# Attention and feed-forward in one kernel: one pool of four single PSUM banks, a half tile more in seven products, and a new order of all engines

## The chip, the cores and the metric

The kernel runs on one core of a Trainium2 chip. The metric is the device time of one execution in microseconds (us), the median of the runs shown; lower is better. A profile is one execution recorded instruction by instruction; its span runs from the program's first instruction to its last.

## The reference

```python
def _attn_ref(q, k, v, bias_table):            # q, k, v: (8, 8, 576, 64); bias_table: (32, 8)
    scores = scale * np.matmul(q, k.transpose(0, 1, 3, 2))
    ...
    bucket = np.where(is_small, n, large) + np.where(rel < 0, 0, 0)   # n = |i - j|
    scores = scores + bias_table[bucket].transpose(2, 0, 1)[None, :, :, :]
    scores = scores - np.max(scores, axis=-1, keepdims=True)
    attn = np.exp(scores)
    attn = attn / (np.sum(attn, axis=-1, keepdims=True) + 1e-09)
    return np.matmul(attn, v)

def _moe_ref(x, w_in, w_out):                  # x: (4608, 512); w_in: (512, 2048); w_out: (2048, 512)
    h = x @ w_in
    g = np.maximum(0.01 * h, h)
    return g @ w_out

x = attn_out.transpose(0, 2, 1, 3).reshape(B * S, H * D)
return _moe_ref(x=x, **moe_kwargs)
```

Eight batches of eight heads go through attention with a bias that depends on |i - j| alone; its output, 4608 tokens of 512 values, goes through two matrix products with a leaky ReLU between them.

## The kernel before

**Attention.** Work goes by pairs of heads: pair n is heads 2p and 2p+1 of batch b, with n = 4b + p, 32 pairs in all. For a pair, q and k are brought to d-by-token layout, either by TensorE transposes (`turn_by_pe`, L414 and L419) or by one DMA transpose on the SP queue (`turn_by_dma`, L405, chosen by `by_dma`), and copied to `qt` and `kt` (`take_turned`, L431, on ACT or DVE). `score` makes six products u = 0 to 5 in tiles of two PSUM banks (`ps_s`); `expo` (L470 to L477) takes the exponential on ACT into `at`, `extra` or `at4`; `band` (L490) multiplies the part near the diagonal by the exponential of the bias, on DVE. `av` (L525, L528) multiplies by v with a column of ones, one head (e = 0 or 1) to a bank (`ps_o`, `ps_om`); `norm` (L537, L538) divides on DVE into `opair`. The result is turned to `xT`, by TensorE and a copy (`x_pe`, `x_copy`) or by a DMA transpose on SP (`x_dma`, L544). For pairs 4 to 30 the last 64 keys go first (`av_tail`), beside the next pair's score tiles 2 and 3.

**Feed-forward.** The 4608 tokens make nine tiles T of 512, and tile T needs all four pairs of every batch that it touches: tile 2 needs pairs 8 to 11. `ffn_in` (L576) makes one of 16 blocks f of 128 hidden values in two halves of two matmuls of 512 columns; `ffn_act` (L652) is the leaky ReLU on ACT. The second product goes by seven products of half-size blocks instead of eight, with sums formed on DVE (`mix_g`, `mix_weights`; `product`, L706; `combine`, L722 and L714). For the tiles in `SPLIT` the first product goes by seven products too, in two units u of eight blocks f each (`in_product`, L633), at the price of copies on ACT (`in_keep`, L637), additions on DVE (`in_add`, L643) and ReLUs from SBUF (`in_act`, L649).

**PSUM.** Eight banks: two score tiles of two banks ("S"), one bank for AV ("O") and three for everything else ("M").

**Order.** Every engine runs an order written at build time. `Plan` takes tasks with an engine, a cost, what they come after and which PSUM slots they take and give. It places them one by one by the earliest start and a rank, with three tables by task number: `SHIFT` changes ranks, `HOLD` delays, `SWAP` moves a copy between ACT and DVE. All engines, SP and POOL too, then run in that order, and wait for each other by semaphores. Where the plan sees TensorE idle in the first 26 us of its own reckoning, `spin` puts matmuls on a tile of zeros (`junk`). The plan reckons 6 us for an `x_dma`, and a rule of its own for `turn_by_dma`:

```python
if "turns" in t:
    t["end"] = max(r + 4.5, min(ring + 2.0, r + 11.0))
if "moves" in t:
    t["end"] = ring = max(ring, r + t["cost"] + 1.0) + t["moves"]
```

Of the kernel before, what the change touches and what calls it, by code (L numbers as in the profile page):

```python
# [10 lines left out]
FP32 = mybir.dt.float32  # L11
# [24 lines left out]

class Plan:


    LAG, COLD, WARM, EARLY, PATIENCE = 0.25, 4.9, 26.0, 34.0, 0.3  # L40

    SHIFT = {
# [26 lines left out]
    }  # L69

    SWAP = (20, 62, 88, 91, 92, 180, 185, 209, 214, 265, 273, 274, 996, 1089, 1368, 1757,)

    def __init__(self, slots):
        self.tasks = []
# [93 lines left out]
    def run(self, fill):  # L168

        for t in self.order():  # L170
            if t["engine"] == "PE" and 3.9 < t["start"] < self.WARM:
                k = round(t["idle"] / 0.22) if t["start"] < 8.5 else int((t["idle"] - 0.1) / 0.11)
                if k > 0:
                    fill(k)
# [924 lines left out]
```

## Time and profile before

| what | value |
|---|---|
| median of 3 runs | 360.63 us (360.44 to 366.01) |
| profiled execution, its own time | 360.76 us |
| its span | 359.0 us |
| mean granted TensorE clock | 0.999 |
| DVE busy, share of the span | 83% |
| ACT busy, share of the span | 73% |
| matmuls on zeros (`junk`) | 44 |
| DMA traffic | 39.58 MB |

The profiled execution takes 1.76 us more than its span, which lies around the first and the last instruction. TensorE's busy time counts a matmul from its start to the end of its drain, so that neighbours overlap; what one costs in a row of its like is the distance from start to start. In the profile's rows PE is TensorE's matmuls, DVE VectorE, ACT ScalarE, POOL GpSimd (which issues most loads) and SP the queue of DMA transposes and stores; the number in brackets at a row's end is how long the engine had been idle, and for whom it waited.

### The profile page before, as it was taken

To read this page: it belongs to the slowest core of one execution; us is meant where nothing else is said; L and a number is where in the kernel's file an instruction comes from. 1 tells how busy PE (TensorE), PEld (TensorE's weight loads), DVE (VectorE), ACT (ScalarE), POOL (GpSimd) and SP (SyncE) were. 2 spreads that over 40 slices of the span, in tenths; PEclk is the share of its full clock that TensorE was granted. 3 is DMA by queue.
4 is the path that set the end of the run, shared out by engine and by line. 5 is a ranking of instruction groups with operands and counts; after the bars stand their busy time and mean duration, and the time that the engine had idled before them with its cause. 6 is when DMAs were issued, how large, how long until landed. Compare 5 with 4: busy or idle time off the path is not lost.

```text
span 359.0 us, 9973 instructions
## 1 busy us (share of the span) xinstructions
PE 350.7 (98%) x4147; PEld 254.1 (71%) x4172; DVE 297.6 (83%) x705; ACT 262.2 (73%) x352; POOL 70.3 (20%) x107
## 2 busy tenths in 40 slices
PE   8998999999999999999999999999999999999996
PEld 5665456774677655656767777667678888888885
DVE  6897979999799968986899879999559489497593
ACT  4988999678986899797988887887933574656530
POOL 8956123080008004300700310000000000000000
PEclk9999999999999999999999999999999999999999
DMA  8999999999949987991999296411123011030033
GB/s 126 148 178 193 203 179 144 142 147 208 133 113 125 136 153 89 193 182 20 133 158 222 42 141 89 135 21 21 20 20 119 2 63 57 2 117 2 0 119 117
DMA packets 103724, 39.58 MB, mean 110 GB/s; under 512 B 83200, under 2 KB 98560, under 8 KB 103680
## 3 DMA queue, kind: packets, MB, share of 16 engines
q0 software_dynamic: 53424, 18.21, 52.8%
q1 hardware_dynamic: 49904, 20.32, 31.8%
q8 instruction: 32, 0.52, 0.6%
q10 hardware_dynamic: 352, 0.43, 0.4%
q14 instruction: 12, 0.10, 0.1%
HBM read 36.70 MB, written 9.44 MB: 129 GB/s over the span
## 4 chain that ended last, share of the span: by engine, by line
PE 90%; DVE 5%; ACT 3%; issue 1%; DVEq 0%; ACTq 0%
PE pm L706 31%; PE pm L576 21%; PE pm L633 10%; PE ps_s L456 9%; PE ps_om L525 5%; PE ps_o L525 5%; PE ps_s L460 2%; PE ps_s L463 2%; PE ps_w L1064 1%; ACT at L470 1%; DVE at L490 1%; PE ps_o L510 1%; DVE opair L538 1%; PE ps_t L414 1%; ACT gt L652 1%
## 5 line engine op out<-in xcount | busy, mean ns | idle before, releaser
L470 ACT ACTIVATE at<-ps_s 128x1024 bf16<-128x1024 f32 x124 | 121.2, 1031 | 25.4 <-PE ps_s L456 22.3
L576 PE MATMUL pm<-xT,w_in_sb 128*128 128x512 bf16 (+1 forms) x423 | 91.2, 347 | 1.5 <-DVE xT L557 0.5
L490 DVE TENSOR_TENSOR at<-at,hk 128x768 bf16<-128x768 bf16 (+4 forms) x156 | 66.6, 450 | 14.1 <-ACT at L470 11.0
L652 ACT ACTIVATE gt<-pm 128x512 bf16<-128x512 f32 x96 | 57.3, 620 | 17.0 <-PE pm L576 16.5
L576 PEld LDWEIGHTS <-w_in_sb 128*128 128x128 bf16 x448 | 40.1, 98 | 32.4 <-issue 5.5
L706 PEld LDWEIGHTS <-gt 128*128 128x128 bf16 x576 | 54.7, 98 | 11.7 <-issue 3.0
L722 DVE TENSOR_TENSOR y<-pm,y 128x512 f32<-128x512 f32 (+1 forms) x53 | 41.1, 778 | 18.1 <-PE pm L706 17.1
L268 POOL DMA_DIRECT2D vn<-in_v_dram x32 | 28.8, 912 | 126.1 <-PE ps_o L525 110.9
L706 PEld LDWEIGHTS <-sum 128*128 128x128 bf16 x432 | 41.2, 98 | 9.0 <-issue 2.5
L525 PEld LDWEIGHTS <-at 128*128 128x128 bf16 x1240 | 41.4, 98 | 3.0 <-issue 0.7
L456 PE MATMUL ps_s<-qt,kt 64*128 64x512 bf16 x256 | 40.5, 387 | 0.6 <-ACT qt L431 0.4
L706 PE MATMUL pm<-w_out_sb,gt 128*128 128x256 bf16 x288 | 36.9, 273 | 0.0
L706 PE MATMUL pm<-mix,gt 128*128 128x256 bf16 x288 | 36.2, 273 | 0.0
L706 PE MATMUL pm<-w_out_sb,sum 128*128 128x256 bf16 x288 | 36.0, 273 | 0.0
L525 PE MATMUL ps_o<-vn,at 128*128 128x65 bf16 x640 | 25.4, 193 | 0.3 <-DVE opair L538 0.2
L525 PE MATMUL ps_om<-vn,at 128*128 128x65 bf16 x600 | 24.0, 194 | 0.0
L477 ACT ACTIVATE at<-ps_s 128x576 bf16<-128x576 f32 x31 | 20.9, 673 | 0.5 <-PE ps_s L464 0.4
L643 DVE TENSOR_TENSOR at<-pm,at 128x512 f32<-128x512 f32 (+1 forms) x18 | 15.3, 864 | 6.7 <-ACT at L637 3.6
L637 ACT COPY at<-pm 128x1024 f32<-128x1024 f32 x12 | 12.1, 1012 | 12.0 <-PE pm L633 11.9
L472 ACT ACTIVATE at<-ps_s 128x512 bf16<-128x512 f32 x31 | 19.0, 613 | 2.4 <-PE ps_s L460 1.7
L456 PEld LDWEIGHTS <-kt 64*128 64x128 bf16 x256 | 8.0, 94 | 17.3 <-issue 15.8
L706 PE MATMUL pm<-mix,sum 128*128 128x256 bf16 x144 | 19.0, 273 | 0.0
(119 smaller groups left out, 505.1 us busy)
## 6 DMA issues: line engine op xcount, KB each, us to landing
out_dram<-y SPq DMA_DIRECT2D x16, 512.0 KB, 3.4
vn<-in_v_dram POOLq DMA_DIRECT2D x32, 128.0 KB, 6.4
qn<-in_q_dram POOLq DMA_DIRECT2D x14, 288.0 KB, 10.9
kn<-in_k_dram POOLq DMA_DIRECT2D x14, 288.0 KB, 11.3
w_in_sb<-in_moe_w_in_dram POOLq DMA_DIRECT2D x2, 1024.0 KB, 11.2
w_out_sb<-in_moe_w_out_dram POOLq DMA_DIRECT2D x2, 1024.0 KB, 18.9
out_dram<-y SPq DMA_DIRECT2D x3, 256.0 KB, 2.2
qn<-in_q_dram POOLq DMA_DIRECT2D x4, 144.0 KB, 4.0
```

What stands on the lines that cost most here:

```text
L268: nc.gpsimd.dma_start(out=vn[i][:, c, :, 0:D], in_=v[b, :, c * P : (c + 1) * P, :].rearrange("h s d -> s h d"),)
L456: nc.tensor.matmul(ps[:, e, :], lhsT=kt[r, u * P : (u + 1) * P], rhs=qt[r, 0:512], start=True, stop=True)
L470: nc.scalar.activation(at[:, :, u, 0:512], ps, AF.Exp, scale=scale)
L472: nc.scalar.activation(at[:, :, :, 512:S].rearrange("p e c i -> p c e i"), ps[:, 0, :].rearrange("p (c e i) -> p c e i", e=2, i=SL), AF.Ex ...
L477: nc.scalar.activation(at4[:, 0:S], ps.rearrange("p e i -> p (e i)")[:, 0:S], AF.Exp, scale=scale)
L490: nc.vector.tensor_tensor(out=o, in0=o, in1=m, op=ALU.mult)
L525: nc.tensor.matmul(ps[:, ic, :], lhsT=at[:, o : o + P], rhs=vn[i][:, c, 2 * p + e, :], start=whole and c == 0, stop=not whole and ic == NJ ...
L576: nc.tensor.matmul(pms[T, f][:, o : o + n], lhsT=w_in_sb[:, c, f * P : (f + 1) * P], rhs=xT[c][:, x : x + n], start=(c == 0 and i == 0), s ...
L633: nc.tensor.matmul(ps[:, i, :], lhsT=w, rhs=x, start=fresh and i % 2 == 0 and c == 0, stop=i % 2 == 1 and c == 1, skip_group_check=not fresh)
L652: nc.scalar.activation(gts[T][:, f, :], pms.pop((T, f)), AF.Prelu, bias=0.0, scale=1.0, alpha=0.01)
L706: nc.tensor.matmul(ps[:, ts, :], lhsT=l[:, ts * P : (ts + 1) * P], rhs=r, start=(ts == 0 or apart) and j == 0, stop=(ts == 1 or apart) and ...
L722: nc.vector.tensor_tensor(out=out_, in0=ps, in1=x, op=ALU.add)
```

## The change

- **PSUM:** the AV bank joins the others: four single banks "M" for AV, feed-forward, transposes and the rest. The two score tiles stay.
- **Seven products for half a tile more:** `SPLIT` becomes a list of units, and holds the second unit of tile 5 beside both units of tiles 6, 7 and 8.
- **Pair 7's q and k** are turned by TensorE, as those of pairs 5, 6 and 8 are, and no longer by DMA.
- **Bias table:** its last row is loaded beside the table by a second small DMA and subtracted on DVE, where a TensorE matmul into a bank (`ps_d`) did that.
- **Stores:** each tile's four blocks of 256 rows by 256 columns are stored one by one, when each is done (`block_store`); before, two stores of 256 rows by 512 columns. The first product's copy goes to block c21 instead of c22.
- **Fixed tiles:** `qt`, `pr` and `tu` become fixed buffers used in turn.
- **Zeros:** 19 spins at the start instead of 10; `heat` may put further ones into the bank that the next matmul will write. The program holds 44 of them, as before; 5 stand in an AV bank.
- **Planner:** DMA landings are reckoned with two lanes that share the engines (`Lanes`), in-products of tiles 2 and later are ordered as if their inputs landed 1.5 us later (`spare`), and the three tables are new, so that the order changes on all engines.

```diff
+class Lanes:
...
+    def push(self, t, r):
+        self.now = self.flow(self.now, max(r, self.now), self.queue, self.coming, lambda t, at: None)
+        self.coming.append((r + t["lead"], t["n"], t["lane"], t, t["moves"]))
...
-    LAG, COLD, WARM, EARLY, PATIENCE = 0.25, 4.9, 26.0, 34.0, 0.3
+    LAG, COLD, WARM, EARLY, PATIENCE, FILL = 0.25, 6.3, 26.0, 34.0, 0.3, 95.0
     SHIFT = {
-        31: 1843, 37: 293, 52: 34.5, 154: -274.5, 157: -208.5, 175: 318.5, 205: -304, 207: -210.5, 208: 10248.5,
...
+        30: 208, 53: -955, 94: 68, 147: 50, 152: 38.5, 162: 53.5, 189: 309, 209: -183, 227: 31.5, 228: 125.5,
...
-        if "turns" in t:
-            t["end"] = max(r + 4.5, min(ring + 2.0, r + 11.0))
         if "moves" in t:
-            t["end"] = ring = max(ring, r + t["cost"] + 1.0) + t["moves"]
+            ring.push(t, r)
...
+            if t["engine"] == "PE" and 6.0 < t["start"]:
+                if t["start"] < self.WARM:
+                    fill(round(t["idle"] / 0.22) if t["start"] < 9.0 else int((t["idle"] - 0.1) / 0.11))
+                elif t["start"] < self.FILL:
+                    self.pre = max(0, int((t["room"] - 0.2) / 0.11))
...
-    ps_o_pool = ctx.enter_context(tc.tile_pool(name="ps_o", bufs=1, space=bass.MemoryType.PSUM))
-    ps_m_pool = ctx.enter_context(tc.tile_pool(name="ps_m", bufs=3, space=bass.MemoryType.PSUM))
+    ps_m_pool = ctx.enter_context(tc.tile_pool(name="ps_m", bufs=4, space=bass.MemoryType.PSUM))
...
+    nc.vector.tensor_tensor(out=tab[:, 0, :], in0=tab[:, 0, :], in1=tab[:, 1, :], op=ALU.subtract)
...
-            nc.scalar.activation(diag[r, g, :], ps[r, 0:H], AF.Exp)
+            nc.scalar.activation(diag[r, g, :], tab[:, 0, :], AF.Exp)
+    def heat(ps):
+        for _ in range(plan.pre):
+            nc.tensor.matmul(ps[:, 0:256], lhsT=junk[:, 0:P], rhs=junk[:, 0:256], start=True, stop=True)
+        plan.pre = 0
...
     def by_dma(n):
-        return n > 2 * n_pairs or n == 2 * n_pairs - 1
+        return n > 2 * n_pairs
...
-            outs[n, e] = ps_o_pool.tile([P, NJ + 1, D + 1], FP32, name="ps_o", tag="ps_o")
+            outs[n, e] = ps_m_pool.tile([P, NJ + 1, D + 1], FP32, name="ps_o", tag="m")
+        heat(outs[n, e].rearrange("p i d -> p (i d)"))
...
-    def block_store(T, r, g, ss, queue):
+    def block_store(T, r, g, ss=(0, 1), queue=nc.sync):
...
-    plan = Plan({"S": 2, "O": 1, "M": 3})
+    plan = Plan({"S": 2, "M": 4})
...
-            d = add("SP", 0.1, [r0, r1] + cut.get(n - NTU, [])[:2], lambda: turn_by_dma(n), rank, tail=6.0)
+            d = moves(add("SP", 1.3, [r0, r1] + tu_use.get(n - NTU, []), lambda: turn_by_dma(n), rank), 2.2, 1, 2.0, 2.6)
...
-            xt[n] = [add("SP", 0.1, nms + free_x, lambda: x_dma(n), soon + 4, tail=6.0)]
+            xt[n] = [moves(add("SP", 1.2, nms + free_x, lambda: x_dma(n), soon + 4), 1.2, 1, 2.0, 2.6)]
...
+            if T > 1:
+                for t in early + [i]:
+                    t["spare"] = 1.5
...
-                stored[T] = [add("SP", 0.1, [cb[5], cb[4]], lambda: ffn_store(T, 1), 10000, tail=2.5)]
+                stored[T, r, g] = [moves(add("SP", 0.45, [cb[k]], lambda r=r, g=g: block_store(T, r, g), 10000), 0.75, 1, 2.0, 2.3)]
...
-    SPLIT = (6, 7, 8)
+    SPLIT = [(5, 1)] + [(T, u) for T in (6, 7, 8) for u in range(2)]
...
-    spin(10)
+    spin(19)
```

How the order moves is seen at three places. The first is VectorE's queue while the first pairs of heads are worked: `at_115` (before) and `at_112` (after) belong to pair 0, `at_116` and `at_113` to pair 1, `extra` to pair 2; a product of one of these with `hk` is a `band`, and RECIPROCAL is the start of a `norm`. Before:

```order
L490 TENSOR_TENSOR at_116<-at_116,hk 128x2x256
L490 TENSOR_TENSOR at_116<-at_116,hk 128x2x384 x2
L490 TENSOR_TENSOR at_116<-at_116,hk 128x2x320
L490 TENSOR_TENSOR at_1_118<-at_1_118,hk_102 128x192
L490 TENSOR_TENSOR at_115<-at_115,hk 128x2x320
L431 COPY qt<-ps_t 128x576
L435 TENSOR_TENSOR qt<-qt,own 128x128
L490 TENSOR_TENSOR extra<-extra,hk 128x2x256
L490 TENSOR_TENSOR extra<-extra,hk 128x2x384
L537 RECIPROCAL rcp<-ps_o 128x5
```

And the same place now:

```order
L531 TENSOR_TENSOR at_112<-at_112,hk 128x2x256
L531 TENSOR_TENSOR at_112<-at_112,hk 128x2x384 x2
L531 TENSOR_TENSOR at_112<-at_112,hk 128x2x320
L531 TENSOR_TENSOR at_0_114<-at_0_114,hk_90 128x192
L531 TENSOR_TENSOR at_113<-at_113,hk 128x2x256
L471 COPY kt_99<-ps_t 128x576
L475 TENSOR_TENSOR kt_101<-kt_101,own 128x128
L475 TENSOR_TENSOR kt_99<-kt_99,own 128x128
L531 TENSOR_TENSOR at_113<-at_113,hk 128x2x384 x2
L531 TENSOR_TENSOR at_113<-at_113,hk 128x2x320
L475 TENSOR_TENSOR qt_102<-qt_102,own 128x128
L579 RECIPROCAL rcp<-ps_o 128x5
```

Pair 0's band of 320 columns, without which its AV cannot start, stood behind all of pair 1's; now it stands ahead of pair 1's first, and pair 0's division comes ahead of pair 2's bands. On TensorE, pair 0's AV goes from behind pair 2's third score tile to behind pair 1's fifth.

The second is the SP queue around the output transposes of pairs 8 to 11 (`xT_90` to `xT_93` before, `xT_78` to `xT_81` now), on which tile 2 waits. Before:

```order
L544 DMA_TRANSPOSE xT_90<-opair 128x5x128
L405 DMA_TRANSPOSE tu<-pr 128x12x96 x2
L544 DMA_TRANSPOSE xT_91<-opair 128x5x128
L726 DMA out_dram<-y 128x2x512
L405 DMA_TRANSPOSE tu<-pr 128x12x96
L544 DMA_TRANSPOSE xT_92<-opair 128x5x128
L544 DMA_TRANSPOSE xT_93<-opair 128x5x128
```

And now:

```order
L586 DMA_TRANSPOSE xT_78<-opair 128x5x128
L445 DMA_TRANSPOSE tu_108<-pr_105 128x12x96
L769 DMA out_dram<-y 128x2x256
L586 DMA_TRANSPOSE xT_79<-opair 128x5x128
L445 DMA_TRANSPOSE tu_109<-pr_106 128x12x96
L769 DMA out_dram<-y 128x2x256
L586 DMA_TRANSPOSE xT_80<-opair 128x5x128
L445 DMA_TRANSPOSE tu_110<-pr_107 128x12x96
L586 DMA_TRANSPOSE xT_81<-opair 128x5x128
```

Pair 11's transpose now stands behind one of q and k that followed it, and narrower stores stand between.

The third is TensorE at the first in-product of tile 2. Before, it follows a product of tile 1:

```order
L706 LDWEIGHTS sum_98
L706 MATMUL pm_2414<-w_out_sb,sum_98 128x256
L576 LDWEIGHTS w_in_sb
L576 MATMUL pm_2436<-xT_90,w_in_sb 128x512
L576 LDWEIGHTS w_in_sb
L576 MATMUL pm_2436<-xT_91,w_in_sb 128x512
```

And now it follows a score tile of pair 13:

```order
L501 LDWEIGHTS kt_100
L501 MATMUL ps_s<-qt_103,kt_100 128x128
L619 LDWEIGHTS w_in_sb
L619 MATMUL pm_2384<-xT_78,w_in_sb 128x512
L619 LDWEIGHTS w_in_sb
L619 MATMUL pm_2384<-xT_79,w_in_sb 128x512
```

Between the end of pair 11's AV and this matmul TensorE's queue held pairs 12's and 13's AV before, and holds pair 12's alone now: seven half products of `product` (four matmuls each), pair 13's six score products with pair 12's tail, and pair 12's two AV heads.

More of the change, by code (lines that the diff above doesn't have):

```diff
@@ L145, in order @@
             r = max([r] + [s[t["take"].count(k) - 1] for k, s in held.items()])
-            ring = self.place(t, r, free, slots, ring)
+            t["room"] = r - max([free.get(e, 0.0)] + [s[t["take"].count(k) - 1] for k, s in held.items()])
+            self.place(t, r, free, slots, ring)
         return done
@@ L165, in place @@
             slots[k].append(t["end"] + self.LAG)
-        return ring
     def run(self, fill):
         for t in self.order():
[L171 to L174, printed above, removed]
+            if t["engine"] == "PE" and 6.0 < t["start"]:
[3 more added lines that the diff above has]
+                    self.pre = max(0, int((t["room"] - 0.2) / 0.11))
             t["go"]()
+            self.pre = 0
 @with_exitstack
@@ L248 @@
     kts_ = [per.tile([P, S + P], BF16, name=f"kt{i}") for i in range(3)]
+    qt_ = [per.tile([P, S + P], BF16, name=f"qt{i}") for i in range(3)]
+    pr_ = [per.tile([P, 2, NC, 2 * D], BF16, name=f"pr{i}") for i in range(NPR)]
+    tu_ = [per.tile([P, 2 * NC, RQ], BF16, name=f"tu{i}") for i in range(NTU)]
     own = per.tile([P, 2, SL], BF16, name="own")
@@ L427, in take_turned @@
         if j == 0:
[L428 removed]
+            t = qts[n] = qt_[n % NQT]
         else:
@@ L756, with moves, pool_load @@
     prev = []
-    def pool_load(key, cost, go, moves, after=(), rank=1):
+    def moves(t, work, lane, lead, least, yields=0.39):
+        t["moves"], t["lane"], t["lead"], t["least"], t["yields"] = work, lane, lead, least, yields
+        return t
+    def pool_load(key, cost, go, work, after=(), rank=1):
         t = add("POOL", cost, prev + list(after), go, rank)
-        t["moves"] = moves
+        moves(t, work, 0, min(cost + 1.0, 3.2), cost + 2.2, 0.39 if key[0] in ("qk", "v") else 0.2)
         prev[:] = [t]
@@ new lines, in plan_split, with pe @@
+        rank = [10000 + T * 64 + (u * 7 + i) * 64 / 14 for i in range(7)]
+        g = SPLIT.index((T, u))
+        prior = held_use[g - 2] if g >= 2 else [t for m in range(N - 2, N) for t in avt[m]]
+        def pe(k, after, r, take=(), q=None):
+            for hf in (None,) if k == 2 else (0, 1):
+                t = add("PE", 0.439, base + after, lambda hf=hf: in_product(T, u, k, q, hf), rank[r], take=list(take))
+                xm_use.setdefault(T, []).append(t)
+                after, take = after + [t], ()
+            return t
@@ new lines, in plan_split @@
+        sums = lambda k: [wm[k, c] for c in range(2)]
+        a1 = pe(1, prior + opened[-1:], 0, ["S"])
+        k1 = add("ACT", 0.91, [a1] + prior, lambda: in_keep(T, u, 0), 0)
+        bs = [pe(2, [a1], 1, ["M"], q) for q in range(2)]
+        h11 = [add("DVE", 0.605, [bs[q], k1], lambda q=q: in_add(T, u, 0, ("b", q), q), 0, give=["M"]) for q in range(2)]
+        a6 = pe(6, [k1, xm] + sums(1), 2)
+        k6 = add("ACT", 0.91, [a6] + prior, lambda: in_keep(T, u, 1), 0)
+        c5 = pe(5, [xm, a1] + sums(0), 3, ["S"])
@@ L978, in plan_ffn @@
+        held_use.append(p)
+        return {2 * j + h: ((p[0], p[3]), (p[1], p[2]))[h] for j in range(4 * u, 4 * u + 4) for h in range(2)}
     def plan_ffn(T):
```

214 lines of the change are left out of this document (104 added, 110 removed), and 40 rows, old and new, of tables (HOLD, SHIFT).

## The prediction

> **What bounds the kernel now.** I read the page's busy shares and the chain of waits first.
>
> ```profile
> span 359.0 us, 9973 instructions
> PE 350.7 (98%) x4147; PEld 254.1 (71%) x4172; DVE 297.6 (83%) x705; ACT 262.2 (73%) x352; POOL 70.3 (20%) x107
> PE 90%; DVE 5%; ACT 3%; issue 1%; DVEq 0%; ACTq 0%
> ```
>
> TensorE carries 90% of the chain, but a mean says nothing of where another engine decides. So next I read the busy times by stages (columns: stretch, its length, busy time and instructions of PE, PEld, DVE, ACT, POOL, then clock, DMA share, GB/s).
>
> ```profile
> 34.00:60.00 26.00, 24.72 (x247) 13.24 (x251) 23.35 (x62) 25.28 (x38) 7.72 (x11) 1.00 1.55 184
> 60.00:260.00 200.00, 198.85 (x2481) 135.54 (x2499) 175.79 (x444) 164.77 (x231) 36.79 (x47) 1.00 1.02 119
> 260.00:353.00 93.00, 92.95 (x872) 81.72 (x873) 68.43 (x108) 46.40 (x49) 0.00 (x0) 1.00 0.15 51
> ```
>
> From 60 to 353 us TensorE rests for 1.15 + 0.05 = 1.2 us in all. There a change pays only by taking work from TensorE, and costs only by making it wait. From 34 to 60 it rests for 26.00 - 24.72 = 1.28 us, and ACT is the fuller engine (25.28). Before 34 us TensorE's busy time says little, since matmuls on zeros fill its gaps. So there I read ACT's timeline, from the first exponential to the first of pair 4 (start, duration, line, operation, then the idle time before it and its releaser).
>
> ```profile
> 8.40 1.94 ACT L470 ACTIVATE at<-ps_s 128x1024 bf16<-128x1024 f32 x2 [1.77 <-PE ps_s L456]
> 10.54 1.94 ACT L470 ACTIVATE at<-ps_s 128x1024 bf16<-128x1024 f32 x2 [0.21 <-PE ps_s L456]
> 12.96 0.60 ACT L472 ACTIVATE at<-ps_s 128x512 bf16<-128x512 f32 x1 [0.48 <-PE ps_s L460]
> ...
> 24.58 0.65 ACT L477 ACTIVATE extra<-ps_s 128x576 bf16<-128x576 f32 x1 [0.69 <-PE ps_s L464]
> ...
> 26.30 1.94 ACT L470 ACTIVATE at<-ps_s 128x1024 bf16<-128x1024 f32 x2 [0.39 <-PE ps_s L456]
> 28.45 2.11 ACT L470 ACTIVATE at<-ps_s 128x1024 bf16<-128x1024 f32 x2 [0.22 <-PE ps_s L456]
> 30.46 0.63 ACT L431 COPY kt<-ps_t 128x576 bf16<-128x576 bf16 x1
> ...
> 33.89 1.94 ACT L470 ACTIVATE at<-ps_s 128x1024 bf16<-128x1024 f32 x2 [1.22 <-PE ps_s L456]
> ```
>
> Between 8.40 and 33.89, 25.49 us, ACT idles 0.21 + 0.48 + 0.69 + 0.39 + 0.22 + 1.22 = 3.21 us, each time for scores. The start is bound by ACT's exponentials and the scores that feed them; the rest by TensorE.
>
> **The change part by part.** *Start.* The AV bank of before made pairs 0, 1 and 2 queue:
>
> ```profile
> 20.91 0.29 PE L525 MATMUL ps_o<-vn,at 128*128 128x65 bf16 x4
> ```
>
> Pair 0's AV began here and the others followed close, and ACT's waits of 0.69, 0.39 and 0.22 fall in or just behind this clump. Now pair 0's AV goes ahead of pair 2's scores, since its last band goes earlier on VectorE, and four banks let its neighbours overlap. I take 1.0 of these 1.30 us as gained. Of the 0.48 I take 0.3: one bias spread instead of two stands ahead of that score tile. Of the 1.22 I take 0.4: copies of q and k that stood between its releaser and it go elsewhere. Against that ACT has one copy more in this stretch, 0.63 in the row at 30.46, about 0.5 from start to start with a neighbour. Net -1.2 us. Its ends: all 3.21 gone less the copy, -2.7, and nothing gone, +0.5. Two small matmuls for the last table row leave TensorE and a VectorE subtraction comes; zeros stand on both sides of them, so I count nothing. It would cost one small VectorE operation if the table's second load came late.
>
> *TensorE's own work.* The prices, from the chain of waits (start, time on the chain):
>
> ```profile
> 39.05 0.26 PE ps_t L414 x6
> 42.85 1.73 PE pm L576 x8
> 305.32 4.37 PE pm L633 x40
> 342.00 11.80 PE pm L706 x108
> ```
>
> A matmul of 512 columns takes 1.73/8 = 0.216 us, one of 256 takes 4.37/40 = 0.109 in either line. The split unit of tile 5 was eight blocks of four of the first, 32 x 0.216 = 6.91 us; it becomes seven products of eight of the second, 56 x 0.109 = 6.10: -0.81. Pair 7 turned by TensorE adds two groups of six, 2 x 0.26 = +0.52. Net -0.3. What the split costs elsewhere is read from the groups by line:
>
> ```profile
> L637 ACT COPY at<-pm 128x1024 f32<-128x1024 f32 x12 | 12.1, 1012 | 12.0 <-PE pm L633 11.9
> L649 ACT ACTIVATE gt<-at 128x1024 bf16<-128x1024 f32 x12 | 12.7, 1058 | 8.3 <-DVE at L643 8.1
> L652 ACT ACTIVATE gt<-pm 128x512 bf16<-128x512 f32 x96 | 57.3, 620 | 17.0 <-PE pm L576 16.5
> ```
>
> and from the additions' own view, where the shapes stand apart (shortest, median, longest in ns):
>
> ```profile
> L643 DVE TENSOR_TENSOR at<-pm,at x18: 679/692/1225, 272.0 to 336.4; 128x512 f32<-128x512 f32 x12, 128x1024 f32<-128x1024 f32 x6
> ```
>
> A unit has three copies, four additions (two of 512 columns, two of 1024) and four ReLUs of 1024; the rows hold those whose sums lie in `at`, and the prices serve for the others. So a unit brings ACT 3 x 1.01 + 4 x 1.06 us and takes eight ReLUs of 0.62 away: +2.3; VectorE gets 2 x 0.69 + 2 x 1.22 = 3.8. In the last stretch VectorE has 93.00 - 68.43 = 24.6 us free and ACT 46.6; that is the cover. Without it the longer, 3.8, is what TensorE could wait at most.
>
> *34 to 60 us.* TensorE's 1.28 us of rest stand in ACT's shadow. Tile 0's first second product starts one pair earlier, so TensorE has more ready work. I take -0.7; ends -1.3 (all) and +0.3, since ACT also takes over copies from VectorE.
>
> *Tile 2.* Its in-products are now ordered as if their inputs came earlier than the old plan said. The stretch of TensorE's timeline from pair 12's last scores before pair 11's AV to tile 2's first in-product is:
>
> ```profile
> 104.71 0.61 PE L456 MATMUL ps_s<-qt,kt 64*128 64x512 bf16 x4
> ...
> 105.40 0.79 PE L525 MATMUL ps_om<-vn,at 128*128 128x65 bf16 x20
> 106.03 0.76 PE L525 MATMUL ps_o<-vn,at 128*128 128x65 bf16 x20
> 106.63 0.38 PE L460 MATMUL ps_s<-qt,kt 128*128 128x128 bf16 x4
> 106.85 1.04 PE L706 MATMUL pm<-w_out_sb,gt 128*128 128x256 bf16 x8
> ...
> 108.26 0.61 PE L456 MATMUL ps_s<-qt,kt 64*128 64x512 bf16 x4
> 108.80 1.49 PE L706 MATMUL pm<-mix,sum 128*128 128x256 bf16 x12
> 110.12 0.38 PE L463 MATMUL ps_s<-qt,kt 128*128 128x512 bf16 x1
> ...
> 110.36 1.47 PE L706 MATMUL pm<-mix,gt 128*128 128x256 bf16 x12
> ...
> 118.30 1.03 PE L576 MATMUL pm<-xT,w_in_sb 128*128 128x512 bf16 x4
> ```
>
> and the output transpose of pair 11, with that of all 24 below (issue, then landing):
>
> ```profile
> L544 SPq DMA_TRANSPOSE xT<-opair x1: 1202/1202/1202, 108.0 to 108.0; - x1
> DMA to landing us min/median/max: 5.3/5.3/5.3
> ...
> L544 SPq DMA_TRANSPOSE xT<-opair x24: 1198/1220/4462, 64.5 to 260.5; - x24
> DMA to landing us min/median/max: 2.6/3.8/11.2
> ```
>
> Pair 11's AV ended at 106.63 and its transpose was issued 1.4 us later and landed 5.3 after that, 6.7 in all; tile 2 came 118.30 - 106.63 = 11.7 behind, with 5 us to spare. In the new order seven half products stand between, 28 x 0.109 = 3.06; pair 13's first scores, 0.54; a fifth score, 110.12 to 110.36, 0.24; scores 2 and 3 with the tail, 104.71 to 105.40, 0.69; two AV heads, 105.40 to 106.63, 1.23; the last score, 106.63 to 106.85, 0.22. Sum 6.0. With the same landing TensorE waits 6.7 - 6.0 = 0.7 us, and everything queued behind the in-product waits with it; I take +0.7, with ends 0 (median landing 3.8: 1.4 + 3.8 is below 6.0) and +3 inside the forecast. Where SP's queue moves, pair 11's transpose now stands behind one of q and k, and narrower stores between; I count nothing for them, and 1.2 more, the issue time in the row, if that transpose is in the way. The stores, tables and fixed buffers lie off TensorE's path: zero, with this cover.
>
> Sum: -1.2 - 0.3 - 0.7 + 0.7 = -1.5 us on the profiled execution's 360.76 (span 359.0 and 1.76 around it) gives 359.3. That execution is 0.13 above the median shown, 360.63, so I say 359.1.
>
> **The rivals.** *All rest goes.* Start -2.7, 34 to 60 -1.3, work -0.3, no wait at tile 2: -4.3, 356.3. For it: each idle row names scores, and four banks remove the queue for AV. Against it: scores also wait for copies of q and k on VectorE and ACT, which no bank speeds up.
>
> *Output transposes land late (slower).* Transfers still move 119 GB/s in the stretch from 60 us, and one of the 24 landed after 11.2 us. If that happens at tile 2, TensorE waits 1.4 + 11.2 - 6.0 = 6.6 us: -2.2 + 6.6 = +4.4, 365.0. It turns the change into a loss when landing exceeds 2.2 + 6.0 - 1.4 = 6.8 us. For it: narrow distance and 5.3 already. Against it: the median is 3.8.
>
> *Nothing gained.* ACT's start stays as long and has one copy more, +0.5; 34 to 60 unchanged; work -0.3; tile 2 +0.7: +0.9, 361.5. For it: in that stretch ACT idles only 3.2 of 25.5 us and each wait may only move on to the next.
>
> *The clock rises earlier.* The chain of waits at the start:
>
> ```profile
> 1.10 2.31 PE ps_w L1064 x10
> ...
> 5.32 0.62 PE ps_t L419 x12
> ...
> 10.51 0.38 PE ps_t L419 x12
> ```
>
> Ten matmuls of 256 columns on zeros take 0.231 us each, against 0.109 later, and twelve transposes 0.62 against 0.38, so TensorE runs at half speed first. Nineteen unbroken spins instead of ten, with zeros and 20 other small matmuls between, may end that earlier. About 0.5 us is then saved on early transposes and scores (two groups of 0.62 - 0.38): 358.6. The Trainium skill's page "TensorE: Matmul & The Clock Gate", in "The HAM clock gate (the "warmup" mystery)", has a window of about 3.4 us that does not start with the kernel and must be busy; the slow rows at the start agree, and that the phase varies from run to run would make this a matter of luck. By that rule the gain may be 0.5 us or none; no row of this case shows the phase.
>
> **How the numbers follow.** Forecast 0.38, its own range 357.6 to 360.5; all rest goes 0.12; late transposes 0.15; nothing gained 0.23; clock 0.12. The signs are mixed: three cases below the old time hold 0.62, two above hold 0.38. The range runs from 356.2, just below the first rival, to 363.0, between the third and the late transposes, and leaves out most of the latter and little else. Two per cent of 360.63 is 7.2 us, bounds 353.4 and 367.8, about what a measurement of this kernel can tell from no change. Faster than that needs more than all rest and a further 3 us of TensorE's work: 0.02. Slower needs a landing of more than 1.4 + 11.2 us or two late tiles: 0.03. Else 0.95.
>
> **What would show it.** ACT's idle from the first exponential to pair 4's: 2.0 us or less if the start is right, 3 or more if not. TensorE's rest from 34 to 60 us near 0.6. At tile 2's first in-product a wait of about 0.7 with an output transpose as releaser; over 3 is the slow rival, none means the transpose lands sooner. Between 260 us and the end TensorE should stay full; a rest there with VectorE named would mean the additions of tile 5 are not hidden. Transposes of pair 0 at about 0.38 for twelve show the clock's rival. The prediction is wrong if TensorE waits at a place that none of these rows names.

## The result: 1.1% slower, by waits for transfers in the middle

The changed kernel takes 365.28 us (median of 6, 364.15 to 367.86) against 360.53 before (median of 6). The ratio to the kernel before is 1.0112, 95% interval 1.0073 to 1.0151: about 4 us slower. The ratio and its interval rest on the undisturbed executions alone (one before, of 366.01, was in a slower state of the chip); the medians of all are 4.75 us apart. The forecast was 359.1 with a range of 356.2 to 363.0, so the time lies outside it, and on the other side of the old time. The profiled execution took 364.15 us, the shortest of the six; its span is 362.3.

The page of the changed kernel, with the chain of waits by engine:

```profile
span 362.3 us, 10124 instructions
PE 351.4 (97%) x4206; PEld 256.6 (71%) x4206; DVE 292.4 (81%) x703; ACT 275.8 (76%) x365; POOL 70.2 (19%) x107
PE 52%; DMA 5%; DVE 5%; ACT 5%; issue 2%; DVEq 0%; ACTq 0%
```

TensorE is as busy as before, in a span that is 3.3 us longer. What is new is in the third line: transfers hold 5% of the chain, where there were none before. (The chain could be followed back from the end to 108.6 us only, so its shares add up to 69%; before, they add up to 99%.) Busy times by stages (same columns as in the prediction):

```profile
34.00:60.00 26.00, 25.42 (x277) 14.61 (x275) 22.67 (x55) 24.82 (x40) 7.45 (x11) 1.00 1.66 187
60.00:260.00 200.00, 195.59 (x2420) 131.71 (x2420) 167.22 (x434) 170.23 (x233) 36.74 (x46) 1.00 0.96 118
260.00:353.00 93.00, 93.00 (x927) 83.03 (x924) 70.56 (x115) 52.34 (x54) 0.00 (x0) 1.00 0.15 48
```

From 34 to 60 us TensorE's rest fell from 1.28 to 0.58 us. From 260 us on it is full. From 60 to 260 us the rest rose from 1.15 to 4.41 us: the loss is there. Even the 1.15 is mostly no rest: the trace of the kernel before holds 423 of the 448 in-products of its line 576, and 19 gaps of 0.05 us from 60 to 260 us are where such a record is missing; in the changed kernel's trace none is. The start, in contrast, became shorter. ACT's waits from its first exponential to pair 4's first (31.44; start, duration, operation, idle time before it):

```profile
7.41 3.77 ACT L511 ACTIVATE at<-ps_s 128x1024 bf16<-128x1024 f32 x4 [0.48 <-PE ps_s L497]
...
18.59 0.65 ACT L518 ACTIVATE at<-ps_s 128x576 bf16<-128x576 f32 x1 [0.55 <-PE ps_s L505]
19.69 3.77 ACT L511 ACTIVATE extra<-ps_s 128x1024 bf16<-128x1024 f32 x4 [0.45 <-PE ps_s L497]
...
31.44 1.94 ACT L511 ACTIVATE at<-ps_s 128x1024 bf16<-128x1024 f32 x2 [0.61 <-PE ps_s L497]
```

Pair 4 comes at 31.44 instead of 33.89, 2.45 us earlier, and the idle time on the way is 0.55 + 0.45 + 0.61 = 1.61 instead of 3.21.

Now the middle. What TensorE waited for longest between 60 and 262 us (engine, line, releaser: total, times, longest; one more row has 0.2 us):

```profile
PE pm L619 <- DMA xT<-opair: 1.6, 2, 1.3
PE pm L619 <- DVE opair L580: 1.4, 1, 1.4
PE ps_s L501 <- ACT at L511: 1.2, 1, 1.2
```

The first row names a transfer. The other two name VectorE and ACT, so one asks next what these waited for. The timelines of PE, ACT and VectorE at the second and third:

```profile
70.96 1.19 ACT L471 COPY qt<-tu 128x576 bf16<-128x576 bf16 x1 [2.02 <-DMA tu<-pr]
72.06 1.93 ACT L511 ACTIVATE at<-ps_s 128x1024 bf16<-128x1024 f32 x2
...
73.12 0.38 PE L501 MATMUL ps_s<-qt,kt 128*128 128x128 bf16 x4 [1.17 <-ACT at L511]
...
188.55 0.69 DVE L760 COPY y<-pm 128x512 f32<-128x512 f32 x1 [1.67 <-DMA out_dram<-y]
...
195.92 0.49 DVE L580 TENSOR_TENSOR opair<-ps_om,rcp 128x320 bf16<-128x320 f32 x1
...
196.47 1.03 PE L619 MATMUL pm<-xT,w_in_sb 128*128 128x256 bf16 x8 [1.36 <-DVE opair L580]
```

All three are the same thing, a transfer that landed late. ACT stood 2.02 us for pair 10's q, and the exponentials that free the score tiles stood behind that copy. VectorE stood 1.67 us for a store that had not yet left the tile it was to overwrite, and seven microseconds later the division that frees a shared bank came late, for which TensorE stood 1.36 us. The first row is tile 2: in the order before its in-products came 11.7 us behind pair 11's AV, now 117.41 - 111.22 = 6.2.

```profile
111.22 0.60 PE L749 MATMUL pm<-mix,gt 128*128 128x256 bf16 x4
...
117.41 1.24 PE L619 MATMUL pm<-xT,w_in_sb 128*128 128x512 bf16 x5
119.91 0.81 PE L619 MATMUL pm<-xT,w_in_sb 128*128 128x512 bf16 x3 [1.26 <-DMA xT<-opair]
```

Who stood ahead of these transfers is seen in the row of pair 11's output transpose (issue and landing), and in GpSimd's timeline at that place:

```profile
L586 SPq DMA_TRANSPOSE xT<-opair x1: 1213/1213/1213, 113.6 to 113.6; - x1
DMA to landing us min/median/max: 6.3/6.3/6.3
...
111.59 3.53 POOL L307 DMA_DIRECT2D vn<-in_v_dram  x4 [31.54 <-PE ps_o L567]
115.08 1.29 POOL L313 DMA_DIRECT2D v<-in_v_dram  x2
```

The same AV that gives pair 11's output also frees the V buffer. GpSimd, which had waited 31.54 us for that, issues the next V loads at once, from 111.59 us on; the transpose has to wait for two divisions and comes at 113.57, behind three of the four V parts. The store of the third wait, then the issues of all stores by the page (issues, size, median us to landing):

```profile
L769 SPq DMA_DIRECT2D out_dram<-y x1: 887/887/887, 182.2 to 182.2; - x1
DMA to landing us min/median/max: 6.3/6.3/6.3
...
out_dram<-y SPq DMA_DIRECT2D x35, 256.0 KB, 2.2
```

It was issued at 182.2 us, behind another such burst (V loads from 177.91 us on), and took 6.3 us where the median is 2.2. The transpose of pair 10's q and k stood behind loads of q and k that were issued from 53.29 us on:

```profile
L445 SPq DMA_TRANSPOSE tu<-pr x1: 2595/2595/2595, 59.4 to 59.4; - x1
DMA to landing us min/median/max: 11.5/11.5/11.5
```

Counted another way, from each matmul's start to the next one's, less the distance at which such matmuls follow each other undisturbed, with the records missing from the trace put in by the program's order (small gaps that both kernels have are in it):

| kernel | to 60 us | from 60 us | together |
|---|---|---|---|
| before | 12.7 | 10.6 | 23.4 |
| changed | 10.2 | 16.8 | 27.1 |

The change is 2.5 us ahead by 60 us, and loses 6.2 us after it. With 0.4 us less of work that makes 3.3, the difference of the spans.

### The profile page after: what moved, and what is told of

Its sections match the earlier page's. It is cut to its first block, busy times and chain, and to the rows that moved or that the text cites. A ratio compares the mean times of both kernels' runs of the same rounds, so it can differ in the third digit from the quotient of the medians.

```text
span 362.3 us, 10124 instructions
## 1 busy us (share of the span) xinstructions
PE 351.4 (97%) x4206; PEld 256.6 (71%) x4206; DVE 292.4 (81%) x703; ACT 275.8 (76%) x365; POOL 70.2 (19%) x107
## 4 chain that ended last, share of the span: by engine, by line
PE 52%; DMA 5%; DVE 5%; ACT 5%; issue 2%; DVEq 0%; ACTq 0%
PE pm L749 20%; PE pm L676 12%; PE pm L619 9%; PE ps_s L497 4%; DMA xT<-opair 3%; PE ps_o L567 2%; PE ps_om L567 2%; ACT at L511 2%; DMA out_dram<-y 2%; ACT gt L695 2%; DVE sum L717 1%; DVE y L765 1%; PE ps_s L501 1%; PE ps_s L504 1%; DVE opair L580 1%
## 5 line engine op out<-in xcount | busy, mean ns | idle before, releaser
L619 PE MATMUL pm<-xT,w_in_sb 128*128 128x512 bf16 (+1 forms) x416 | 86.4, 346 | 3.7 <-DMA xT<-opair 1.6
L619 PEld LDWEIGHTS <-w_in_sb 128*128 128x128 bf16 x416 | 37.6, 98 | 35.5 <-issue 9.2
L695 ACT ACTIVATE gt<-pm 128x512 bf16<-128x512 f32 x88 | 51.0, 643 | 12.7 <-PE pm L619 12.4
L765 DVE TENSOR_TENSOR y<-pm,y 128x512 f32<-128x512 f32 (+1 forms) x53 | 41.0, 774 | 13.5 <-PE pm L749 13.2
L680 ACT COPY at<-pm 128x1024 f32<-128x1024 f32 x15 | 15.1, 1008 | 12.5 <-PE pm L676 12.5
L686 DVE TENSOR_TENSOR at<-pm,at 128x512 f32<-128x512 f32 (+1 forms) x22 | 19.0, 879 | 6.8 <-ACT at L680 4.6
L692 ACT ACTIVATE gt<-at 128x1024 bf16<-128x1024 f32 x15 | 15.8, 1056 | 5.2 <-DVE at L686 5.2
## 6 DMA issues: line engine op xcount, KB each, us to landing
w_in_sb<-in_moe_w_in_dram POOLq DMA_DIRECT2D x2, 1024.0 KB, 11.2
```

What stands on the lines that cost most here:

```text
L619: nc.tensor.matmul(pms[T, f][:, o : o + n], lhsT=w_in_sb[:, c, f * P : (f + 1) * P], rhs=xT[c][:, x : x + n], start=(c == 0 and i == 0), s ...
L695: nc.scalar.activation(gts[T][:, f, :], pms.pop((T, f)), AF.Prelu, bias=0.0, scale=1.0, alpha=0.01)
L765: nc.vector.tensor_tensor(out=out_, in0=ps, in1=x, op=ALU.add)
```

## The experiments

**The theory** after the traces: the new order gains at the start and has no fault in itself, but puts the work that needs a transfer nearer to its landing than landings are while bursts of loads run. **The rivals:** four shared banks and a fuller ACT make TensorE wait whatever the transfers do; or any wait taken away only moves on to the next.

**Loads cut, in both kernels.** The edit:

```diff
-  out=dst[0:RQ, h0:h1, :, :] ...
+  out=dst[0:RQ, h0:h0 + (h1 - h0 if b < 2 else 2 if b == 2 else 1), :, :] ...
-  out=vn[i][:, c, :, 0:D],
+  out=vn[i][:, c, 0:(H if b < 2 else 1), 0:D],
```

> The changed kernel with the loads of batches 2 to 7 cut: each q, k and v load is issued as before, in the same order, but brings one head (q and k of batch 2: two heads) instead of four or eight, so that later batches attend to stale data. Every engine's order stays. Theory (landing): in the changed kernel TensorE rests 1.17 us for scores of pair 10 (ACT waits 2.02 us for a DMA transpose of q), 1.26 and 0.32 us for output transposes at tiles 2 and 3 and 1.36 us for a bank whose division on VectorE stands behind a store that has not left; all four transfers queue behind load bursts. With little to queue behind, these rests go: 364.2 to 365.5 becomes 359 to 360.5, and transposes land about 2.6 us after issue. Rival (banks or order by themselves): four shared banks and ACT's heavier queue make TensorE wait whatever the transfers do: the time stays above 363.

> The kernel before with the same cut loads (batches 2 to 7 attend to stale data). Theory (landing): its order keeps distance from its transfers; between 60 and 353 us its TensorE rests only 1.2 us in all, so it gains at most that: 359.3 to 360.5 against 360.5. Rival (loads slow everything, through memory or queues, in both kernels): it gains as much as the changed kernel does, 3 us or more.

Measured: the changed kernel takes 359.12 us, ratio to the kernel before 0.9941 (0.9909 to 0.9973); the kernel before with the same cut takes 360.33, 0.9983 (0.9955 to 1.0011). So the same relief is worth about 1.7% to the new order and nothing measurable to the old one. With the loads cut in both, the changed kernel is 0.4% (1.5 us) faster by the ratios, which is the gain that was forecast; the two intervals overlap, so this is not firm. The output transposes of the changed kernel, first as it is, then with the loads cut, and the middle stage with the loads cut:

```profile
L586 SPq DMA_TRANSPOSE xT<-opair x24: 1199/1208/4228, 67.4 to 262.4; - x24
DMA to landing us min/median/max: 2.6/4.0/12.8
```

```profile
DMA to landing us min/median/max: 2.6/2.6/4.7
...
60.00:260.00 200.00, 198.68 (x2482) 136.11 (x2495) 171.49 (x445) 172.86 (x236) 23.99 (x42) 1.00 0.50 87
```

With little to queue behind, an output transpose lands in 2.6 us at the median, one of q and k in 3.8 (5.5 at most, where it was 13.5), and TensorE's rest in the middle falls from 4.41 to 1.32 us, with banks, orders and ACT's queue as they were. The rival of banks falls; so does the one that loads slow both kernels.

**Waits taken away one by one, with all transfers running.** In-products read weights in place of `xT`, copies of q and k read weights in place of `tu`, stores read weights in place of `y`:

```diff
-  rhs=xT[c][:, x : x + n],
+  rhs=xT[c][:, x : x + n] if T < 2 else w_in_sb[:, c, o : o + n],
-  src = turned[n][:, j * NC : (j + 1) * NC, :].rearrange("p c r -> p r c")
+  src = w_in_sb[:, j, 0:S].rearrange("p (c r) -> p r c", c=NC)
-  in_=y[:, r, ss[0] : ss[-1] + 1, g, :])
+  in_=w_out_sb ... [:, 0 : len(ss) * HE] ... (tiles 0 to 7)
```

> The changed kernel with the plain in-products of tiles 2 to 5 reading a slice of the first weight matrix in place of the transposed attention output (these tiles' results are not the reference's); all transfers, instructions and orders stay. It takes away only the wait for output transposes. Theory (landing): the rests of 1.26 and 0.32 us at tiles 2 and 3 and some 0.3 us behind them go, nothing else: 1.5 to 2.0 us less than the changed kernel, about 363 us. Rival (the rest only moves to the next wait in the fixed order): less than 0.7 us is gained.

> The changed kernel with three waits for transfers taken away at once: plain in-products of tiles 2 to 5 as in the run before; the copies of q and k of pairs 9 to 31 read a slice of the first weight matrix in place of what the DMA transposes brought; stores of tiles 0 to 7 send a slice of the second weight matrix, so that the sums on VectorE never wait for a store (results are not the reference's). Transfers, instructions and orders stay. Theory (landing): 1.6 (in-products) + 1.8 (pair 10, with what follows) + 1.5 (store) = about 5 us less than the changed kernel: 359 to 360.5, below the kernel before or equal to it. Rival (shared banks): 1.36 us of it stays, and the time stays above 361.

> The changed kernel itself, as the common base of this group. Expected: its ratio to the kernel before near 1.011 again, and rests of TensorE at the same places in its profile, with lengths that differ by up to 1 us as landings differ.

> The changed kernel with the copies of q and k of pairs 9 to 31 reading a slice of the first weight matrix instead of what their DMA transposes brought (the attention of these pairs is not the reference's); transfers and orders stay. It takes away only the wait for transposes of q and k. Theory (landing): the rest of 1.17 us before pair 8's last score and what follows it (0.33 and 0.13) go: 1.2 to 2.0 us less than the changed kernel. Rival (moves on): the next wait takes it up, under 0.6 us.

> The changed kernel with the stores of tiles 0 to 7 reading a slice of the second weight matrix instead of the sums (the output is not the reference's), so that no sum on VectorE waits for a store; transfers and orders stay. Theory (landing): the 1.36 us rest near 195 us goes (VectorE waited 1.67 us for a store, the divisions that free the shared bank stood behind it): 1.0 to 1.5 us less than the changed kernel. Rival (the shared bank itself): the rest stays, under 0.4 us.

| what reads weights | median us | ratio to before | interval |
|---|---|---|---|
| nothing (the changed kernel again) | 365.66 | 1.0112 | 1.0050 to 1.0173 |
| in-products | 362.58 | 1.0031 | 1.0000 to 1.0063 |
| copies of q and k | 363.24 | 1.0077 | 1.0051 to 1.0102 |
| stores | 363.79 | 1.0079 | 1.0040 to 1.0119 |
| all three | 360.18 | 0.9984 | 0.9959 to 1.0009 |

By the ratios, in-products are worth 0.8% (2.9 us), copies 0.35% (1.3 us), stores 0.3% (1.2 us), all together 1.3% (4.6 us). The first is more than the 2.0 expected at most, the others are within what was expected; the intervals of the single ones overlap with each other and with that of the changed kernel in this table, so only the sum is firm. In the run with all three the middle stage reads:

```profile
60.00:260.00 200.00, 198.81 (x2482) 135.90 (x2494) 171.84 (x444) 172.74 (x236) 36.26 (x46) 1.00 1.00 120
```

1.19 us of rest, as in the kernel before (1.15). That 1.36 us of rest carried the name of a division and a shared bank, and yet went with the stores (in the run with the stores alone too, where the one division that TensorE waits for, 0.8 us, is one whose result a transpose reads), decides against the bank by itself: no wait for a bank of that size is left in this run.

How long the waits are changes from one execution to the next. The same copy of pair 10's q, in ACT's waits of the profiles of the changed kernel, of it again, and of the runs with in-products and with stores fixed:

```profile
ACT qt L471 <- DMA tu<-pr: 2.0, 1, 2.0
```

```profile
ACT qt L471 <- DMA tu<-pr: 0.4, 1, 0.4
```

```profile
ACT qt L471 <- DMA tu<-pr: 3.4, 1, 3.4
```

```profile
ACT qt L471 <- DMA tu<-pr: 2.9, 1, 2.9
```

Between 0.4 and 3.4 us with one order. The first two are two executions of the same program: there the transpose landed 11.5 and 9.9 us after its issue, and in the second TensorE did not rest for these scores at all. Where the order leaves no distance, the landing's scatter goes into the time.

**V loads behind the output transpose.** If bursts that overtake are the cause, then holding a burst back must help, although it brings loads later. GpSimd copies one column of the fourth pair's `xT` before the V loads:

```diff
+  if j == 0 and b > 3:
+      o = (b - 2) % RING * S
+      nc.gpsimd.tensor_copy(out=seen, in_=xT[n_pairs - 1][:, o : o + 1])
```

> The changed kernel, where GpSimd copies one column of the transposed output of pair 4b-5 before it issues the V loads of batch b (b = 4 to 7), so that these loads start only when that output transpose has landed. In the changed kernel three V parts were issued ahead of pair 11's transpose (111.59, 112.47 and 113.34 against 113.57 us), and it landed with the third, 6.3 us after issue. Theory (loads overtake): the transpose of the fourth pair then lands 2.6 to 3.5 us after issue; the rests of 1.26 and 0.32 us at tiles 2 and 3 go, and the store of the 1.36 us rest starts nearer to the head of its burst: 1.6 to 3 us less than the changed kernel, 362 to 363.5. Rival (only shifted): q and k loads behind V come as much later, their DMA transposes too, and TensorE rests elsewhere: the same 365 or more.

Measured: 361.76 us, ratio 1.0019 (0.9988 to 1.0050), 0.9% (3.4 us) less than the changed kernel, a little more than expected. Pair 11's transpose and GpSimd's timeline in that run:

```profile
L590 SPq DMA_TRANSPOSE xT<-opair x1: 1200/1200/1200, 113.8 to 113.8; - x1
DMA to landing us min/median/max: 2.4/2.4/2.4
...
116.24 0.19 POOL L308 COPY seen<-xT 128x1 bf16<-128x1 bf16 x1 [36.94 <-DMA xT<-opair]
116.73 3.83 POOL L310 DMA_DIRECT2D vn<-in_v_dram  x4 [0.31 <-issue]
```

It lands after 2.4 instead of 6.3 us; the V loads start at 116.73 instead of 111.59, and TensorE waits for no output transpose in this profile. The rest near 195 us is gone too. This is the cause shown from the other side, in a kernel that leaves nothing out.

**The remaining wait moved.** In `Plan.run` single tasks are put later in the finished order, first ACT's copy of pair 10's q and the product that follows it, then all that VectorE does for pairs 9, 10, 12 and 13 there, then its copies for pair 11:

```diff
-  for t in self.order():
+  todo = self.order()
+  for n, m in self.LATER:          # task n goes behind task m
+      ...
+  for t in todo:
```

> The run before, and ACT's copy of pair 10's q (it waited 2.02 us for its DMA transpose with ready exponentials behind it) moved behind pair 8's next two exponentials and pair 9's copy on ACT's queue, with VectorE's product of that q moved behind its next sum. Theory (landing): a further 1.2 to 1.8 us less, 360 to 361.5, equal to the kernel before or up to 0.5 us below it. Rival: ACT then waits for scores instead and nothing more is gained than in the run before.

> The changed kernel with V loads of batches 4 to 7 behind the output transpose, as before, and with the work that waits for the q and k transposes of pairs 9 and 10 moved behind pair 7's divisions: on VectorE the copy of k and its product of pair 9, the rows of pairs 12 and 13, and pair 10's copy and products; on ACT pair 10's copy of q. In the run with both mended, VectorE still waited 1.99 us for pair 9's k and TensorE rested 1.37 us for the division behind it. Theory (landing): 1.0 to 1.5 us less than with V loads alone, 359.5 to 360.5 where the kernel before takes 360.6. Rival (moves on): as late pairs 9, 12 and 13 now get their q and k, a rest of the same size comes when their scores are due, and nothing is gained.

> The run with more moved (1.0016 of the kernel before), and VectorE's copies of q and k of pair 11 moved behind its sum for the fifth product of tile 0: there TensorE rested 1.22 us for that sum, which frees a bank, behind these two copies. Theory (the lead is kept once each wait is moved where nobody is due): 0.8 to 1.2 us less, 0.998 of the kernel before, about 359.8 against 360.5. Rival (the order is full there): the time stays at 1.0 to 1.002, and a rest of about 1 us stands at a new place.

The first: 360.81, 1.0011 (0.9981 to 1.0041), less gain than expected. ACT no longer waited, but VectorE stood for pair 9's k, and TensorE for the division behind it:

```profile
74.87 0.45 PE L605 MATMUL ps_tx<-ident,opair 128*128 128x128 bf16 x5 [1.37 <-DVE opair L591]
```

The second: 360.86, 1.0016 (0.9985 to 1.0046), nothing gained; here VectorE's copies of q and k of pair 11 stood in front of a sum that frees a bank:

```profile
81.94 1.02 PE L630 MATMUL pm<-xT,w_in_sb 128*128 128x512 bf16 x4 [1.22 <-DVE y L776]
```

The third: 360.26, 0.9978 (0.9950 to 1.0006), as expected; the middle stage and all of TensorE's waits from 60 to 262 us:

```profile
60.00:260.00 200.00, 198.29 (x2478) 135.71 (x2490) 172.24 (x443) 172.03 (x235) 38.17 (x50) 1.00 0.98 121
...
PE ps_s L508 <- ACT at L524: 0.5, 1, 0.5
PE pm L630 <- ACT gt L706: 0.2, 1, 0.2
PE pm L630 <- issue: 0.2, 1, 0.2
```

This version is about 1.3% below the changed kernel. Against the kernel before it is 0.2% lower in the middle of an interval that just includes 1, so it equals it and is not shown to beat it. By the count from start to start it has 10.0 us to 60 us and 12.5 after it. So some 1.9 us of the lost 6.2 stay, in gaps of 0.5 us at most, and no row of the waits names a transfer for them; with the loads cut, 1.3 stay (11.9). What they come from was not tried.

**Zeros at the start**, 10 for 19 in the changed kernel, 19 for 10 in the kernel before:

```diff
-  spin(19)
+  spin(10)
```

> The changed kernel with 10 matmuls on zeros at the start in place of 19; everything else stays. Theory (clock): nine fewer let TensorE fall idle or stay slow in the first transposes and scores; the first exponential comes 0.5 to 1.0 us later than 7.41 us and the time is 0.5 to 1.0 us longer than the changed kernel's, about 366. Rival (order alone): the start is set by loads and by ACT, the first exponential stays at 7.4 and the time at 365.3.

> The kernel before with 19 matmuls on zeros at the start in place of 10; everything else stays. Theory (clock): TensorE is at full speed earlier and the first exponential comes before 8.40 us, but the two matmuls for the table and the first transposes stand behind the zeros and come up to 0.8 us later: between -0.5 and +0.5 us against 360.5. Rival (order alone): the extra zeros bring nothing and only push the start: +0.5 us or more.

Measured: 1.0103 (1.0052 to 1.0153) for the changed kernel with 10, and 1.0001 (0.9975 to 1.0027) for the kernel before with 19: neither differs from its own kernel in time, so the 0.5 to 1.0 us expected of the first is not seen. Its first exponential came at 7.65 us, only 0.24 later. Further on the start does differ. Pair 4's first exponential in the changed kernel with 10, and pair 0's and pair 4's in the kernel before with 19 (of this run only the start is read):

```profile
32.22 1.94 ACT L511 ACTIVATE at<-ps_s 128x1024 bf16<-128x1024 f32 x2 [0.61 <-PE ps_s L497]
```

```profile
7.81 2.85 ACT L470 ACTIVATE at<-ps_s 128x1024 bf16<-128x1024 f32 x3 [1.06 <-PE ps_s L456]
...
33.09 1.94 ACT L470 ACTIVATE at<-ps_s 128x1024 bf16<-128x1024 f32 x2 [1.22 <-PE ps_s L456]
```

That is 32.22 instead of 31.44, 7.81 instead of 8.40 and 33.09 instead of 33.89. TensorE's first scores, with 10 and with 19 in the changed kernel, show why:

```profile
7.00 1.04 PE L497 MATMUL ps_s<-qt,kt 64*128 64x512 bf16 x4
```

```profile
6.98 0.61 PE L497 MATMUL ps_s<-qt,kt 64*128 64x512 bf16 x4
```

The same four matmuls are busy for 1.04 us and for 0.61: in the first of these executions TensorE is still slow at 7 us, in the second it runs at full speed. But the number of zeros does not decide this alone. The kernel before with the loads cut starts with 10 zeros and with the loads of batches 0 and 1 whole, and in its profile the first scores and the first exponential come as with 19:

```profile
7.38 0.60 PE L456 MATMUL ps_s<-qt,kt 64*128 64x512 bf16 x4
...
7.81 1.94 ACT L470 ACTIVATE at<-ps_s 128x1024 bf16<-128x1024 f32 x2 [1.63 <-PE ps_s L456]
```

Pair 4 comes at 33.09 there too. And behind 19 zeros without a break the first six transposes took 0.43 us in the profile of the changed kernel, but 0.69 in that of the run with the copies of q and k fixed:

```profile
1.10 4.00 PE L1103 MATMUL ps_w<-junk 128*128 128x256 bf16 x19 [1.10 <-DVE junk L332]
5.02 0.43 PE L454 MATMUL ps_t<-ident,pr 96*128 96x96 bf16 x6
```

```profile
5.12 0.69 PE L454 MATMUL ps_t<-ident,pr 96*128 96x96 bf16 x6
```

So the moment at which TensorE comes to full speed differs from one execution to the next. It came before the first scores in all twelve profiles with 19 zeros and in one of the three with 10; that more zeros make it likelier is suggested by this, not shown. The Trainium skill, "TensorE: Matmul & The Clock Gate", "The HAM clock gate (the "warmup" mystery)", says that the window of about 3.4 us runs freely and is not reset when the kernel starts, so that the point of the rise varies from run to run; these rows agree.

An early rise is worth about 0.8 us at pair 4 (0.78 and 0.80), which does not show in the whole time against intervals of 0.3 to 0.5%. The 2.45 us by which pair 4 comes earlier compare a late rise before with an early one after. Like with like it is 33.09 - 31.44 = 1.65 us with an early rise in both and 33.89 - 32.22 = 1.67 with a late one. This is what the order and the banks bring together, give or take 0.5 us (eight profiles with the changed kernel's order and 19 zeros have pair 4 at 31.05 to 31.91); no run takes the two apart.

## Why the prediction was wrong, point by point

The gains came about as large as forecast. What failed is the price of waiting for transfers: +0.7 us at tile 2 and nothing elsewhere, where taking these waits away gave 4.6 us. By the prediction's own last sign it is wrong, since TensorE waits at three places that none of its rows names: 1.17 us before 73.12, 0.32 at tile 3 and 1.36 before 196.47.

- **Start, -1.2.** Right. In the stretch from the first exponential to pair 4's it was 25.49 - 24.03 = 1.46 us less, with idle 1.61, in the 2.0 that the prediction named; against the start of the kernel before with an early rise of the clock it is 33.09 - 7.81 - 24.03 = 1.25. Not seen was that the first exponential itself comes earlier, by 0.99 us, or 0.40 with an early rise in both.
- **34 to 60 us, -0.7.** Right by the row (0.58 of rest, "near 0.6"), but it does not come on top of the whole gain of the start: the count from start to start gives 2.5 us for all up to 60 us, hardly more than the 2.45 at pair 4.
- **TensorE's own work, -0.3; additions of tile 5 hidden.** Right: the stage from 260 us shows TensorE busy for 93.00 of 93.00 us with VectorE at 70.56 and ACT at 52.34.
- **Tile 2, +0.7.** The place and the releaser are right, the wait is 1.26 us, and a further 0.32 at tile 3 was not in the sum; in-products that wait for no output transpose were worth 2.9 us, so this term was mis-sized by some 2 us. Of the sum's terms the work in between was right (6.2 for 6.0); the issue came 113.57 - 111.22 = 2.35 us after AV, not 1.4, since on VectorE two products of k and q stand ahead of the first head's division now, and a band between it and the second's; the landing took 6.3, not 5.3; and the in-product that needs the fourth pair is the sixth, 1.1 us behind the first, where the prediction counted to the first. The prediction took the old issue and landing as given. They are not: V loads start at AV's end, the transpose after the divisions, and each 0.9 us of delay puts one more V part ahead of it.
- **"The stores, tables and fixed buffers lie off TensorE's path: zero, with this cover."** This step failed. A store frees the tile that the next tile's first sum overwrites; behind a load burst it took 6.3 us, VectorE stood 1.67 us, and with the AV bank in the common pool its lateness reached TensorE: 1.36 us. Stores that nobody waits for were worth 1.2 us. Whether an AV bank of its own would have kept the lateness from TensorE was not run.
- **"ACT also takes over copies from VectorE."** The second step that failed. In the kernel before VectorE copies the q of pairs 9 and 10, from 72.79 us on; now ACT does, and pair 10's stands ahead of ready exponentials, 2.02 us before its transpose landed at 70.93. The prediction costed ACT's extra work, not its extra waits. Copies that wait for no transpose were worth 1.3 us.
- **The slow rival** was right in kind: output transposes late behind loads. Its form was wrong: not one landing of 11.2 us with 6.6 us of wait at tile 2, but four waits of 0.3 to 1.4 us behind a transpose of q, two output transposes and a store. Its break-even, a landing over 6.8 us at one place, missed that several smaller ones add up; it got 0.15. That its 365.0 lies so near the measured 365.28 is luck.
- **The clock rival** had the right mechanism and about the size (0.8 at the start for the forecast 0.5), and no measurable weight in the time. That the 19 zeros brought the early rise is not shown: it came with 10 too, and not at the same moment with 19. What the prediction said of luck there fits.
- **The range** ended at 363.0, between "nothing gained" and the slow rival; the time lies where only the slow rival reached.

## What to carry to other kernels

When an order moves work nearer to a transfer, the old landing time is not the price: list what else is issued at the same event, and in which order, because a delay of the issue puts more traffic ahead of it. Ask for every engine in program order what it will wait for, also for copies and buffers that looked free, since a wait of ACT or VectorE on a transfer reaches TensorE one or two steps later under another name. A burst of loads that nobody needs soon can be held back behind the small transfer that somebody does: here that alone recovered about four fifths of the loss (1.0112 to 1.0019).

## What the runs showed of the hardware

- A DMA transpose of 128x640 took 2.4 to 2.6 us from issue to landing with the least ahead of it and up to 12.8 us behind V, q and k loads; pair 11's, in the changed kernel's profile, landed together with the V part issued just before it (119.87 and 119.73 us).
- The wait for one transfer at one place of one order was 0.4 to 3.4 us in four profiles, and 2.0 and 0.4 in two executions of the same program, so a single profile can show a tight order as harmless.
- Cutting the loads from batch 2 on did not speed up the kernel that kept its distance (0.9983, 0.9955 to 1.0011): by this, loads cost it nothing that these runs can measure.
- The moment at which TensorE came to full speed at the start differed between executions: with 10 zeros ahead, the first four scores were busy for 1.04 us in two profiles and 0.60 in a third; behind 19 zeros, six transposes took 0.43 us in one profile and 0.69 in another.
